# Selecting the routed rows of a sigmoid-attention and mixture-of-depths kernel: by ranks broadcast through DRAM and VectorE scans, in place of matmuls with a selection matrix

## Chip, cores and metric

One core of a Trainium2 chip runs the whole kernel in one launch. The metric is device time in microseconds, the median of several executions. Profiles come from one profiled execution each; its span is the time from the first to the last recorded event.

## What is computed

Attention with a sigmoid in place of the softmax, over 8 batches, 12 heads, 448 tokens and 64 values per head, all fp32. Its output, with the heads laid side by side (768 columns), is the input `x` of a mixture-of-depths block: in each batch the 128 tokens with the highest gate score go through a two-layer network, and the others pass unchanged.

```python
scores = scale * q @ k.T - log(S);  attn = 1 / (1 + exp(-scores));  x = attn @ v
gate = x @ w_gate                                    # per batch: 448 scores
top  = argpartition(-gate, capacity)[:capacity]      # capacity = 128
out  = x.copy()
out[top] = x[top] + sigmoid(gate[top])[:, None] * (relu(x[top] @ w1) @ w2)   # w1 768x1024, w2 1024x768
```

## The kernel before

**Attention.** The 96 heads are cut into 24 groups of four heads; group i belongs to batch i // 3. Two groups make a stage, so there are 12 stages (`s`), and a stage has seven units (`n` from 0 to 6). `turn` transposes raw q and k on VectorE (L184 to L191). `unit(s, n)` computes scores as 32-row by 64-column matmuls into PSUM (L209), and ScalarE evicts them through the sigmoid (L220) in two halves, four banks of PSUM being shared by successive units (`psc`). In a few early units the `o` banks are used instead. `values(s, n)` multiplies the attention weights of stage s by v (L250); its four parts run in the last unit of the stage and in units 0, 1 and 2 of the next one. After the fourth part, `take` transposes each pair of heads on VectorE into the row tile `x_b` (L265).

**The gate.** `gate_part` multiplies a group's rows by `w_gate` and sums (L272, L278). When a batch's three groups are done, `store` writes the row tile to a table `x_d` in DRAM with four transfers on the serial queue SP (L285), and `gate` builds a diagonal form of the scores (L294). `spread` turns that with one matmul by ones into a copy of all 448 scores on every partition (L304, L307) and also brings the scores into a per-token column (L309, L313). `rank` counts, for each token, the higher scores (L321) and the equal ones that stand earlier (L324). `place` adds the two counts (L330) and compares each rank with a row of 0 to 127, which gives a 0/1 matrix `sel` of tokens by slots (L333).

**Selection and routing.** `select` multiplies `sel` by columns that hold token number and score (L340, four matmuls with two result columns), into a spare corner of a score bank. `fetch` copies the token numbers out of PSUM (L345, L347), forms the gate's sigmoid on ScalarE (L349), and issues the gather of 128 rows from `x_d` on GpSimd's queue (L351). `turn_rows` transposes the gathered rows on TensorE (L361) and evicts them (L367). `ffn1` (L377, three pieces per batch, evicted with Relu at L379) and `ffn2` (L386, three pieces, each followed by L388 on VectorE) compute the network, and the result is scattered to the output by GpSimd (L392). `copy_out` copies the table `x_d` to the output on SP (L288).

**Order.** The order on every engine is the order of the program, written out by hand. `routed(b)` enters each batch's steps under a stage and unit in `late`, or in `beside`, which runs the selection inside a unit between its matmuls and its evictions. A batch's last group is computed in stage s - 1, and `spread` stands in unit 4 of stage s (unit 5 for batch 0), ranks in units 4 and 6, the selection in unit 1 or 0 of stage s + 1, and `turn_rows` in unit 3 of that stage. `gap(s, n)` runs the values, then from unit 3 on one waiting piece of `ffn1` or `ffn2` (`go`), and then what is due. After the 12 stages a tail without units finishes batches 6 and 7; `choose` selects there. Loads stand on SP in program order: v for the next stage at unit 0 and behind it up to five of 14 weight pieces at stages 1, 2 and 3 (`load_weights`), q and k at units 0 or 1 and 5. A load whose buffer is still read waits, and with it all that is behind it on SP.

Of the kernel before, what the change touches and what calls it, by code (L numbers as in the profile page):

```python
# [17 lines left out]
def kernel(  # L18
# [11 lines left out]
    nc = tc.nc  # L30
# [33 lines left out]
    head = ctx.enter_context(tc.tile_pool(name="head", bufs=2))  # L64
    dram = ctx.enter_context(tc.tile_pool(name="dram", bufs=2, space=bass.MemoryType.DRAM))
    attnp = ctx.enter_context(tc.tile_pool(name="attnp", bufs=1))
# [33 lines left out]
    def load_v(s):  # L100
# [15 lines left out]
        for n in range(4):  # L116
            nc.sync.dma_start(out=th[n * TT:(n + 1) * TT],
                              in_=blocks(4 * (n // 2), HK + n % 2, 4, 1))

    w1_sb = const.tile([P, KD, F], F32, name="w1_sb")  # L120
    w2_sb = const.tile([P, KF, D], F32, name="w2_sb")

    def load_weights(n0, n1):
        for n in range(max(n0, 0), min(n1, KD + KF)):
            if n < KD:
                nc.sync.dma_start(out=w1_sb[:, n], in_=moe_w1[n * P:(n + 1) * P, :])
            else:
                m = n - KD
                nc.sync.dma_start(out=w2_sb[:, m], in_=moe_w2[m * P:(m + 1) * P, :])
# [8 lines left out]
    earlier = const.tile([P, NC, S], mybir.dt.uint8, name="earlier")  # L138
    iota_r = const.tile([P, CAP], F32, name="iota_r")

    tok_gate = [const.tile([P, NC, 2], F32, name=f"tok_gate{n}") for n in range(2)]
    above = const.tile([P, NC], F32, name="above")
    level = const.tile([P, NC], F32, name="level")
    sel = const.tile([P, NC, CAP], F32, name="sel")

    def constants():
        nc.gpsimd.memset(ones, 1.0)
        make_identity(nc, iden)
        for a in range(4):
            p = slice(a * TT, (a + 1) * TT)  # L150
            nc.gpsimd.dma_start(
                out=wg_b[p],
                in_=bass.AP(tensor=moe_w_gate.tensor, offset=moe_w_gate.offset + a * TT,
                            ap=[[0, TT], [P, HP], [1, TT]]))
        nc.gpsimd.iota(iota_r, pattern=[[1, CAP]], base=0, channel_multiplier=0,
                       allow_small_or_imprecise_dtypes=True)
        for t in (above, level):
            nc.gpsimd.memset(t, 0.0)
        for t in tok_gate:
            nc.gpsimd.memset(t, 0.0)  # L160
            for a in range(4):
                nc.gpsimd.iota(t[a * TT:(a + 1) * TT, :, 0], pattern=[[4, NC]], base=a,
                               channel_multiplier=TB, allow_small_or_imprecise_dtypes=True)
        number = moe.tile([P, TB, TT], F32, name="rep")
        nc.gpsimd.iota(number, pattern=[[1, TB], [TB, TT]], base=0, channel_multiplier=0,
                       allow_small_or_imprecise_dtypes=True)
        for c in range(NC):
            nc.gpsimd.tensor_scalar(
                out=earlier[:, c, :], in0=number.rearrange("p r t -> p (r t)"),
                scalar1=tok_gate[0][:, c, 0:1], scalar2=None, op0=ALU.is_lt)  # L170

# [21 lines left out]
    def unit(s, n):  # L193
# [11 lines left out]
        for e in range(2):  # L205
            for y, (x, r) in enumerate(parts):
                for h in range(4):
# [5 lines left out]
                        start=(e == 0), stop=(e == 1))  # L213
        more = beside.pop((s, n), [])
        for fn, args in more:
            fn(*args, psc[0][:, 0, S:])
        for pr in range(2):
            a = attnp.tile([P, 2, S], F32, name=f"attn{pr}", bufs=NU + 3)
            attn[s, pr, n] = a
            nc.scalar.activation(a, psc[pr][:, :, :S], AF.Sigmoid, bias=bias_s, scale=QK_SCALE)  # L220
            if pr == 0:
                for fn, args in more:
                    fetch(*args, psc[0][:, 0, S:])

# [34 lines left out]
    def take(s, pr, x):  # L259

        b, g = divmod(2 * s + x, NG)
        if g == 0 and pr == 0:
            x_tiles[b] = rows_p.tile([P, TB, HP, TT], F32, name="x_b")
            gate_parts[b] = rows_p.tile([P, TB, NG], F32, name="gate_p")
        nc.vector.transpose(x_tiles[b][:, :, 2 * g + pr, :],  # L265
                            outs[s][x][:, pr, :S].rearrange("p (r t) -> p r t", t=TT))


    def gate_part(i):
# [8 lines left out]
        nc.vector.tensor_reduce(out=gate_parts[b][:, :, g], in_=tmp, axis=AX.X, op=ALU.add)  # L278

    def store(b):  # L280
        x_d = dram.tile([S, D], F32, name="x_d")
        st[b] = dict(x_d=x_d)
        view = x_d.rearrange("(t r) (h a d) -> a t r h d", r=TB, a=4, d=TT)
        for a in range(4):
            nc.sync.dma_start(out=view[a], in_=x_tiles[b][a * TT:(a + 1) * TT])  # L285

# [13 lines left out]
    def spread(b, where="o"):  # L300

        tg = tok_gate[b % 2]
        ps = banks(where)[:, 0, :S]
# [6 lines left out]
        for a in range(4):  # L310
            p = slice(a * TT, (a + 1) * TT)
            n = len(range(a, TB, 4))
            nc.vector.tensor_copy(tg[p, :n, 1], rep_t[p, a:TB:4, 0])  # L313
        st[b]["rep"] = rep

    def rank(b, c):
        tg, rep = tok_gate[b % 2], st[b]["rep"]
        n = P if c < NC - 1 else LAST
        own = tg[:n, c, 1:2]
        junk = moe.tile([P, S], F32, name="scr")  # L320
# [6 lines left out]

    def place(b):
        pl = moe.tile([P, NC], F32, name="place")
        nc.vector.tensor_add(pl, above, level)  # L330
        for c in range(NC):
            n = P if c < NC - 1 else LAST
            nc.vector.tensor_scalar(out=sel[:n, c], in0=iota_r[:n], scalar1=pl[:n, c:c + 1],  # L333
                                    scalar2=None, op0=ALU.is_equal)

    def select(b, s0, n, pk):

        tg = tok_gate[b % 2]
        for c in range(NC):
            nc.tensor.matmul(pk[:n, 0:2], sel[:, c, s0:s0 + n], tg[:, c, :],  # L340
                             start=(c == 0), stop=(c == NC - 1))

    def fetch(b, s0, n, pk):
        row = moe.tile([P, 1], I32, name="row", bufs=2)
        nc.vector.tensor_copy(row[:n], pk[:n, 0:1])  # L345
        idx = moe.tile([P, 1], I32, name="idx", bufs=2)
        nc.vector.tensor_scalar_add(idx[:n], pk[:n, 0:1], float(b * S))  # L347
        gt = moe.tile([P, 1], F32, name="gate", bufs=2)
        nc.scalar.activation(gt[:n], pk[:n, 1:2], AF.Sigmoid)  # L349
        xe = moe.tile([P, D], F32, name="xe", bufs=2)  # L350
        nc.gpsimd.indirect_dma_start(  # L351
            out=xe[:n], out_offset=None, in_=st[b]["x_d"][:, :],
            in_offset=bass.IndirectOffsetOnAxis(ap=row[:n, 0:1], axis=0))
        st[b].update(idx=idx, gate=gt, xe=xe)
# [56 lines left out]
    late = {}  # L411
    beside = {}

# [7 lines left out]
    def routed(b):  # L421

        s = (NG * b + NG - 1) // 2 + 1
        put(late, s, 5 if b == 0 else 4, spread, b)
        for c in range(NC - 1):
            put(late, s, 6 if b == 0 else 4, rank, b, c)
        put(late, s, 6, rank, b, NC - 1)
        put(late, s, 6, place, b)
        if s == NS:
            return  # L430
        put(late, *((s + 1, 1) if b == 0 else (s, 6)), copy_out, b)
        for s0, n in SLOTS:
            if s + 1 < NS:
                put(beside, s + 1, 1 if b == 0 else 0, select, b, s0, n)
            put(late, s + 1, 3, turn_rows, b, n)
            put(late, s + 1, 3, routed_groups, b, n)

    def gates(i):
        gate_part(i)
        b, g = divmod(i, NG)  # L440
        if g == NG - 1:
            store(b)
            gate(b)

    def gap(s, n):
# [13 lines left out]
        due(late, s, n)  # L459
        if n == 3 and s > 0:  # L460
            gates(2 * s - 1)

    def stream():
# [3 lines left out]
        load(1)  # L467
        nc.vector.memset(sel, 0.0)
        nc.vector.memset(bias_s, NEG_LOG_S)
# [4 lines left out]
        for _ in range(3):  # L474
            nc.tensor.matmul(warm[:, 0], sel[:, 0, :], sel.rearrange("p c n -> p (c n)"),  # L475
                             start=True, stop=True)
        constants()
        for s in range(NS):
            for n in range(NU):
# [4 lines left out]
                if n == 0:  # L484
                    load_v(s + 1)
                    load_weights(5 * s - 5, 5 * s)
                if s == 0 and n == 1:
# [3 lines left out]
                gap(s, n)  # L491
                if n == NU - 2:
                    turn(2 * s + 2)
                    load(2 * s + 4)

        def choose(b):
            for s0, n in SLOTS:
                pk = banks("psc")[:, 0]
                select(b, s0, n, pk)
                fetch(b, s0, n, pk)  # L500

        choose(B - 2)
        for n in range(5):
            gap(NS, n)
        for n in range(3):
            go("any")
        due(late, NS, NU - 1)
        choose(B - 1)
        copy_out(B - 1)
        while len(ready) > 1:  # L510
            go("any")
# [3 lines left out]
        while ready:  # L515
            go("any")
        assert not late and not beside

# [31 lines left out]
```

## Time and profile before

| | |
|---|---|
| Median of 3 runs | 490.42 us (489.97 to 491.16) |
| Profiled execution | 489.37 us |
| Its span | 487.6 us |
| TensorE matmuls busy | 470.9 us (97%) |
| VectorE, ScalarE, GpSimd busy | 211.7, 189.4, 28.0 us |
| DMA | 68.67 MB, mean 141 GB/s |
| Scores L209 in `psc` / values L250 with raw_v | 150.3 / 134.7 us |
| `ffn1` L377 / `ffn2` L386 in the `o` banks | 81.7 / 73.4 us |
| Selection L340 | 64 records, 8.3 us |
| `sel` L333 on VectorE | 32 instructions, 7.6 us |
| Gather L351, issue to landing | median 4.5 us |
| Table L285, issue to landing | median 6.7 us, 32 issues |

Shares are of the span. fp32 matmuls appear as two records each. "PEld" is the loading of weights into TensorE, which overlaps its matmuls. The chain of work that ended last goes back from the last instruction to what released each step; it says where a saved microsecond would shorten the execution. The row of granted clock shows in tenths of full speed what the clock gate let TensorE have. A DMA's time to landing counts from its issue to the completion that others wait for.

### The profile page before, as it was taken

To read this page: it belongs to the slowest core of one execution; us is meant where nothing else is said; L and a number is where in the kernel's file an instruction comes from. 1 tells how busy PE (TensorE), PEld (TensorE's weight loads), DVE (VectorE), ACT (ScalarE), POOL (GpSimd) and SP (SyncE) were. 2 spreads that over 40 slices of the span, in tenths; PEclk is the share of its full clock that TensorE was granted. 3 is DMA by queue.
4 is the path that set the end of the run, shared out by engine and by line. 5 is a ranking of instruction groups with operands and counts; after the bars stand their busy time and mean duration, and the time that the engine had idled before them with its cause. 6 is when DMAs were issued, how large, how long until landed. Compare 5 with 4: busy or idle time off the path is not lost.

```text
span 487.6 us, 14593 instructions
## 1 busy us (share of the span) xinstructions
PE 470.9 (97%) x6662; PEld 309.5 (63%) x6662; DVE 211.7 (43%) x461; ACT 189.4 (39%) x253; POOL 28.0 (6%) x45
## 2 busy tenths in 40 slices
PE   8998999499999999999999999999999999999995
PEld 3554646386568465577567476568576667489994
DVE  4315296508252168268152156456433355184101
ACT  4746464223442453544352552543343445011010
POOL 8000000000000000010000000010000000001000
PEclk9999999789999999999999999999999999999999
DMA  8929298985463078498262075658632036165000
GB/s 264 198 83 336 107 311 137 304 249 104 176 152 109 3 166 155 169 221 202 99 153 99 13 173 95 223 131 167 214 82 82 35 59 172 34 97 182 14 34 32
DMA packets 117277, 68.67 MB, mean 141 GB/s; under 512 B 95648, under 2 KB 108000, under 8 KB 116960
## 3 DMA queue, kind: packets, MB, share of 16 engines
q1 hardware_dynamic: 115808, 61.35, 49.0%
q0 software_dynamic: 1408, 6.39, 4.3%
q8 instruction: 52, 0.85, 0.7%
q14 instruction: 9, 0.07, 0.0%
HBM read 53.58 MB, written 25.17 MB: 161 GB/s over the span
## 4 chain that ended last, share of the span: by engine, by line
PE 85%; issue 4%; DMA 3%; DVE 3%; SPq 2%; ACT 1%; POOLq 0%; DVEq 0%; ACTq 0%
PE o L250 24%; PE psc L209 24%; PE o L377 16%; PE o L386 13%; SPq L285 2%; PE o L209 2%; DMA x_d<-x_b 1%; PE psc L386 1%; DMA xe<-x_d,row 1%; PE psc L340 1%; PE o L304 1%; PE o L361 1%; PE o L475 1%; DVE x_b L265 1%; PE psc L377 1%
## 5 line engine op out<-in xcount | busy, mean ns | idle before, releaser
L220 ACT ACTIVATE attn<-psc,bias_s 128x896 f32<-128x896 f32 x158 | 151.1, 1003 | 130.6 <-PE psc L209 117.3
L209 PE MATMUL psc<-qT,kT 32*64 32x448 f32 x2528 | 150.3, 540 | 1.9 <-ACT attn L220 1.9
L250 PE MATMUL o<-attn,raw_v 32*64 32x448 f32 x2304 | 134.7, 536 | 0.7 <-ACT o L253 0.7
L209 PEld LDWEIGHTS psc<-qT,kT 32*64 32x64 f32 x2528 | 61.5, 131 | 61.1 <-issue 37.4
L250 PEld LDWEIGHTS o<-attn,raw_v 32*64 32x64 f32 x2304 | 60.3, 132 | 48.6 <-issue 38.8
L377 PEld LDWEIGHTS o<-xeT,w_sb 128*128 128x128 f32 x672 | 78.9, 197 | 10.7 <-issue 7.9
L377 PE MATMUL o<-xeT,w_sb 128*128 128x128 f32 x672 | 81.7, 282 | 0.9 <-ACT xeT L367 0.9
L386 PE MATMUL o<-w_sb,hT 128*128 128x256 f32 x320 | 73.4, 383 | 0.0
L265 DVE STREAM_TRANSPOSE x_b<-o 128x448 f32<-128x448 f32 x48 | 26.9, 618 | 106.9 <-PE o L250 83.7
L386 PEld LDWEIGHTS o<-w_sb,hT 128*128 128x128 f32 x320 | 59.4, 190 | 16.8 <-issue 5.8
L184 DVE STREAM_TRANSPOSE kT<-raw_k 128x384 f32<-128x384 f32 x48 | 24.7, 554 | 30.2 <-DMA raw_k<-in_k_dram 15.0
L388 DVE SCALAR_TENSOR_TENSOR xe<-o,gate,xe 128x256 f32<-128x256 f32 x20 | 9.7, 483 | 51.5 <-PE o L386 51.5
L379 ACT ACTIVATE hT<-o 128x384 f32<-128x384 f32 (+1 forms) x21 | 9.5, 454 | 56.9 <-PE o L377 56.9
L278 DVE TENSOR_REDUCE gate_p<-scr 128x14 f32<-128x896 f32 x24 | 26.1, 1087 | 0.8
L250 PE MATMUL o<-attn,raw_h 32*64 32x448 f32 x384 | 26.4, 534 | 0.0
L272 DVE TENSOR_TENSOR scr<-x_b,wg_b 128x896 f32<-128x896 f32 x24 | 25.6, 1067 | 0.1
L191 DVE STREAM_TRANSPOSE qT<-raw_q 128x896 f32<-128x896 f32 x23 | 24.7, 1074 | 1.9 <-DMA raw_q<-in_q_dram 1.9
L351 POOL DMA_INDIRECT xe<-x_d,row x8 | 7.9, 987 | 297.0 <-DVE idx L347 222.8
L324 DVE SCALAR_TENSOR_TENSOR scr<-rep,tok_gate,earlier 128x448 f32<-128x448 f32 (+1 forms) x32 | 21.8, 683 | 1.1
L321 DVE TENSOR_SCALAR_CACHE_REDUCE scr<-rep,tok_gate 128x448 f32<-128x448 f32 (+1 forms) x32 | 21.4, 669 | 0.9
L309 DVE STREAM_TRANSPOSE scr<-o 128x448 f32<-128x448 f32 x8 | 5.2, 650 | 37.6 <-ACT rep L307 37.6
L253 ACT ACTIVATE o<-bias_s 1x1 f32<-1x1 f32 x36 | 5.9, 165 | 36.8 <-PE o L250 24.9
(56 smaller groups left out, 204.7 us busy)
## 6 DMA issues: line engine op xcount, KB each, us to landing
raw_k<-in_k_dram SPq DMA_DIRECT2D x24, 448.0 KB, 4.6
raw_q<-in_q_dram SPq DMA_DIRECT2D x24, 448.0 KB, 4.5
x_d<-x_b SPq DMA_DIRECT2D x32, 336.0 KB, 6.7
out_dram<-x_d SPq DMA_DIRECT2D x8, 1344.0 KB, 9.0
raw_v<-in_v_dram SPq DMA_DIRECT2D x48, 192.0 KB, 3.9
w_sb<-in_moe_w_dram SPq DMA_DIRECT2D x6, 512.0 KB, 6.1
w_sb<-in_moe_w_dram SPq DMA_DIRECT2D x8, 384.0 KB, 5.2
raw_h<-in_v_dram SPq DMA_DIRECT2D x48, 32.0 KB, 5.5
```

Of the source, the lines that this page charges most:

```text
L184: nc.vector.transpose(kT[i][:, e, :HK], sk[:, e, :HK].rearrange("p (m c) d -> p c m d", c=NF))
L191: nc.vector.transpose(qT[i], sq)
L209: nc.tensor.matmul(psc[h // 2][y * Dh:(y + 1) * Dh, h % 2, :S], kT[2 * s + x][d, e, r:r + 2, :].rearrange("d r t -> d (r t)"), qT[2 * s + ...
L220: nc.scalar.activation(a, psc[pr][:, :, :S], AF.Sigmoid, bias=bias_s, scale=QK_SCALE)
L250: nc.tensor.matmul(o[x][j * Dh:(j + 1) * Dh, pr, :S], w, a[rows, j, :], start=(n == 0 and c == 0), stop=(n == 3 and c == NF - 1))
L265: nc.vector.transpose(x_tiles[b][:, :, 2 * g + pr, :], outs[s][x][:, pr, :S].rearrange("p (r t) -> p r t", t=TT))
L272: nc.vector.tensor_tensor(out=tmp, in0=x_tiles[b][:, :, 2 * g:2 * g + 2, :].rearrange("p r h d -> p r (h d)"), in1=wg_b[:, 2 * g:2 * g + 2 ...
L278: nc.vector.tensor_reduce(out=gate_parts[b][:, :, g], in_=tmp, axis=AX.X, op=ALU.add)
L321: nc.vector.tensor_scalar(out=junk[:n], in0=rep[:n], scalar1=own, scalar2=0.0, op0=ALU.is_gt, op1=ALU.add, accum_out=above[:n, c:c + 1])
L324: nc.vector.scalar_tensor_tensor(out=junk[:n], in0=rep[:n], scalar=own, in1=earlier[:n, c, :], op0=ALU.is_equal, op1=ALU.mult, accum_out=l ...
L377: nc.tensor.matmul(ps[:, f - f0, :n], w1_sb[:, t, f * P:(f + 1) * P], xeT[:, t, :n], start=(t == 0), stop=(t == KD - 1))
L386: nc.tensor.matmul(ps[:n, :ND], st[b]["hT"][:, t, :n], w2_sb[:, t, cols], start=(t == 0), stop=(t == KF - 1))
```

## The change

- `place` keeps only the add. It stores the 448 ranks to a small DRAM tile with GpSimd's queue (128 partitions of four single values) and reads them back from there, the same row to all 128 partitions, into `spot`.
- `select` is no matmul any more. VectorE compares `spot` with the slot number of each partition and sums token numbers (from `number`, int16) and scores (from `rep`) in two scans with an accumulator; then come the copies, the gate and the gather as before, now from SBUF.
- `beside` and `choose` are gone. Ranking and placing stand together in unit 4 (unit 5 for batch 0), the selection in unit 1 of the next stage. Batch 0's `turn_rows` and network begin in unit 4 and not 3.
- `store` is gone: `take` stores each pair of heads as soon as it is transposed, 4 transfers of 448 pieces of 128 B, 16 per stage; `x_d` has three buffers.
- In stage 2, the `turn` for the next stage moves from unit 5 to unit 3, and a `gate_part` from unit 3 to unit 6.
- Weights are loaded 3, 6, 2 and 3 pieces at a time, behind units (1, 0), (1, 5), (2, 0) and (3, 1), and not 5, 5 and 4 at unit 0 of stages 1 to 3.
- Constants on GpSimd change accordingly, and the first matmuls use a zeroed scratch tile of the same width as `sel`.

On TensorE the order of what stays differs only around batches 0 to 4, where pieces of the network fall one unit later or earlier; on GpSimd's queue each batch's two rank transfers stand ahead of its gather, and in the tail ahead of the scatter of batch 5.

```diff
+    WEIGHTS = {(1, 0): (0, 3), (1, NU - 2): (3, 9), (2, 0): (9, 11), (3, 1): (11, KD + KF)}
...
-        more = beside.pop((s, n), [])
-        for fn, args in more:
-            fn(*args, psc[0][:, 0, S:])
...
-            if pr == 0:
-                for fn, args in more:
-                    fetch(*args, psc[0][:, 0, S:])
...
+        rows = st[b]["x_d"].rearrange("(t r) c -> t r c", r=TB)
+        for a in range(4):
+            c = hp * P + a * TT
+            nc.sync.dma_start(out=rows[:, :, c:c + TT],
+                              in_=x_tiles[b][a * TT:(a + 1) * TT, :, hp, :])
...
-    def store(b):
-        view = x_d.rearrange("(t r) (h a d) -> a t r h d", r=TB, a=4, d=TT)
-        for a in range(4):
-            nc.sync.dma_start(out=view[a], in_=x_tiles[b][a * TT:(a + 1) * TT])
...
         nc.vector.tensor_add(pl, above, level)
-        for c in range(NC):
-            n = P if c < NC - 1 else LAST
-            nc.vector.tensor_scalar(out=sel[:n, c], in0=iota_r[:n], scalar1=pl[:n, c:c + 1],
-                                    scalar2=None, op0=ALU.is_equal)
-    def select(b, s0, n, pk):
-        for c in range(NC):
-            nc.tensor.matmul(pk[:n, 0:2], sel[:, c, s0:s0 + n], tg[:, c, :],
-                             start=(c == 0), stop=(c == NC - 1))
+        ranks = dram.tile([NC, P], F32, name="ranks")
+        nc.gpsimd.dma_start(out=ranks.rearrange("c p -> p c"), in_=pl)
+        spot = moe.tile([P, S], F32, name="spot")
+        nc.gpsimd.dma_start(out=spot, in_=bass.AP(tensor=ranks.tensor, offset=ranks.offset,
+                                                  ap=[[0, P], [1, S]]))
+        st[b]["spot"] = spot
+    def select(b, s0, n):
+        picked = []
+        for what in (number.rearrange("p r t -> p (r t)"), st[b]["rep"]):
+            got = moe.tile([P, 1], F32, name="got", bufs=4)
+            junk = moe.tile([P, S], F32, name="scr")
+            nc.vector.scalar_tensor_tensor(
+                out=junk[:n], in0=st[b]["spot"][:n], scalar=slots[s0][:n], in1=what[:n],
+                op0=ALU.is_equal, op1=ALU.mult, accum_out=got[:n, 0:1])
+            picked.append(got)
...
-        for c in range(NC - 1):
-            put(late, s, 6 if b == 0 else 4, rank, b, c)
-        put(late, s, 6, rank, b, NC - 1)
-        put(late, s, 6, place, b)
+        for c in range(NC):
+            put(late, s, 5 if b == 0 else 4, rank, b, c)
+        put(late, s, 5 if b == 0 else 4, place, b)
...
-                put(beside, s + 1, 1 if b == 0 else 0, select, b, s0, n)
-            put(late, s + 1, 3, turn_rows, b, n)
-            put(late, s + 1, 3, routed_groups, b, n)
+            put(late, s + 1, 1, select, b, s0, n)
+            put(late, s + 1, 4 if b == 0 else 3, turn_rows, b, n)
+            put(late, s + 1, 4 if b == 0 else 3, routed_groups, b, n)
...
-        if n == 3 and s > 0:
+        if n == (NU - 1 if s == 2 else 3) and s > 0:
             gates(2 * s - 1)
...
-                if n == NU - 2:
+                if n == (NF if s == 2 else NU - 2):
                     turn(2 * s + 2)
                     load(2 * s + 4)
+                load_weights(*WEIGHTS.get((s, n), (0, 0)))
```

## The prediction

> **What bounds the kernel now.** I read the busy shares first, then the row of granted clock, then TensorE's waits, and last the chain of work that ended last, in order of time.
>
> ```profile
> PE 470.9 (97%) x6662; PEld 309.5 (63%) x6662; DVE 211.7 (43%) x461; ACT 189.4 (39%) x253; POOL 28.0 (6%) x45
> PEclk9999999789999999999999999999999999999999
> ```
>
> TensorE is busy almost all the time at full clock, but for one dip in slices 8 and 9 (85 to 110 us). So only two things count: matmuls that are removed, and stretches in which TensorE waits or runs slowly. Its waits name the dip (columns: us in total, times, longest):
>
> ```profile
> PE o L361 <- DMA xe<-x_d,row: 5.9, 1, 5.9
> ```
>
> TensorE sat idle once, before the first batch's row transposes (L361), for the gathered rows. The chain shows what lay before and after (start us, us, what):
>
> ```profile
> 78.53 7.14 DMA x_d<-x_b
> 85.73 0.81 issue
> 86.54 6.74 DMA xe<-x_d,row
> 93.42 1.53 PE o L361 x6
> 94.97 0.82 ACT xeT L367
> 95.83 6.62 PE o L377 x36
> 102.46 1.69 PE psc L209 x32
> 104.14 4.21 PE o L377 x36
> 108.36 0.75 PE o L304 x2
> ...
> 121.83 1.50 PE psc L209 x31
> 123.33 0.98 PE psc L340 x8
> 124.32 3.19 PE o L250 x64
> ...
> 157.88 3.01 PE o L250 x63
> ```
>
> The table x_d landed at 85.7, the gather at 93.3. The first 36 matmuls after the wait took 6.62 us, the same 36 later 4.21. The clock in steps (stretch, length, busy PE, PEld, DVE, ACT, POOL, granted clock, DMA share, GB/s):
>
> ```profile
> 87.50:90.50 3.00, 0.01 (x2) 0.00 (x0) 2.93 (x5) 1.90 (x2) 0.15 (x1) 1.00 1.09 235
> 90.50:93.40 2.90, 0.00 (x0) 0.01 (x1) 2.80 (x4) 0.00 (x0) 0.00 (x0) 0.51 1.16 222
> 93.40:100.80 7.40, 6.48 (x29) 6.10 (x30) 0.20 (x1) 0.81 (x1) 0.00 (x0) 0.50 1.09 416
> ```
>
> After 3.0 us without matmuls the clock was halved, and stayed so for 10.3 us. The slow part cost (6.62 - 4.21) + (1.53 - 0.66, the transposes in other stages) = 3.3 us on top of the wait. The Trainium skill, "TensorE: Matmul & The Clock Gate", Part 1, lets a halved clock recover after about 3.4 us of busy matmuls; this row shows 7.4 us, and the row is used. By the page the slow part would cost an estimated 1.7 us and the gain below would be 1.6 us smaller.
>
> **Matmuls removed.** Each select (L340, 8 records) takes 0.98 us of the chain, and the value matmuls behind it take 3.19 instead of 3.01 us: 1.16 us per batch for batches 1 to 6. Batch 7's at 446.43 takes 0.79. All lie on the chain, so for batches 1 to 5 nothing can take their place unless the rows come late. They don't: there ranks are placed in unit 4 of one stage and used in unit 1 of the next, over 15 us of units later, and the gather has from unit 1 to unit 3 (9 us by the chain: 1.50 + 2.25 + 1.55 + 2.25 + 1.53) where its landing took 3.9 to 5.4 us. Sum for 1 to 5: **-5.8 us**.
>
> **The new chain: ranks to selection.** In place of the matmuls stands: ranks stored by GpSimd (512 elements of 4 B), read back to 128 partitions (128 rows of 1,792 B), two VectorE scans, a gather. No row of before shows either transfer. Call L the time from the end of the add at L330 to the landed broadcast. Nearest rows (last column: us from issue to landing):
>
> ```profile
> xe<-x_d,row POOLq DMA_INDIRECT x8, 4.5
> out_dram<-xe,idx POOLq DMA_INDIRECT x8, 3.3
> wg_b<-in_moe_w_gate_dram POOLq DMA_DIRECT2D x4, 24.0 KB, 6.2
> ```
>
> Quiet, one transfer of this queue lands in 3.0 us (the scatters after 425 us); under heavy load it took 7.2 (the longest of xe). So L lies between 2 x 3.0 + 0.2 = 6.2 and 2 x 7.2 + 0.2 = 14.6. I take 4.2 for the ranks (3.3, and 0.9 more on GpSimd: 192 pieces of wg_b took it 0.65 us, so 512 may take 1.7) and 3.3 for the broadcast, with 0.3 for semaphores: **L = 7.8**, near the lower end because the serial queue (SP) is stuck then, see below. The skill speaks against such a store: "DMA: Bandwidth & Descriptors", Rules for kernel authors, says a non-contiguous last dimension becomes one descriptor per element. The same page (Anatomy of one DMA) gives some 2.0 us fixed plus bytes, which would make L an estimated 4.5 and the total that of the first rival; no row here has 4-byte pieces.
>
> The scans cost 2 x (0.685 + 0.083, the L324 row with its accumulator read) = 1.5 us, the two small copies and semaphores 0.6: the gather is issued 2.1 us after the broadcast. On VectorE the four L333 instructions (0.87 us) go, so its load hardly moves. Behind the scans, VectorE holds the x_b transposes, and ScalarE, which waits for the gate's scan, holds the next sigmoid evictions: that is the added wait.
>
> **Batch 0.** Ranking moves from stage 2, unit 6 to unit 5, and the transposes before it (turn, 2.4 us) to unit 3, where they take the slot of a gate_part (2.2 us) that goes behind. Ranks began at 71.75 behind turn; now they begin when the copies of spread end (69.6), take 5.7 and the add ends at 75.5. Broadcast at 83.3, gather issued at 85.4. The table is no longer late: pairs are stored as they come, 16 issues per stage. An issue of a small transfer took SP 0.47 us (raw_h, 4 in 1.87), so 7.5 us from 65; batch 0's eight come first and land near 74, ten us before they are needed. Behind them SP waits at the v load for stage 4, whose buffer is freed only at about 85 (it was issued at 86.12 before), so nothing loads the engines between 75 and 85; the copy to the output and the last weights are still behind it. Then the gather meets those loads: 6 us (4.5 to 6.7), landing at 91.4.
>
> TensorE would reach unit 3 at 84.5 (85.6 less the select). ScalarE's evictions resume at 85.1, so unit 3 starts at 86.1, unit 4 at 89.0 (an eviction between two units without filler) and ends at 90.9; transposes from 91.4 to 92.1. Now spread stands ahead of the first ffn1: its diagonal is ready 7.5 us after the x_b transposes begin (86.12 to 93.6 before; now 85.2 to 92.7). Spread to 93.4, ffn1 to 97.65, the second ffn1 4.2 more: 101.85, with the same work done as at 109.11 before: **-7.3 us**. The idle pieces (1.6, 0.9, 0.5, 0.6 us) are each below the 3.0 us after which the clock fell.
>
> **Batches 6 and 7.** No units cover these. Batch 6: the add ends 8.7 us after its spread starts (405.96 to 414.68), the gather lands 8.7 + 7.8 + 2.1 + 3.9 = 22.5 after it, and TensorE comes to L361 at 23.4 - 1.16 = 22.25: -1.16 + 0.25 = **-0.9**. Batch 7: the add ends at 443.2, the broadcast lands at 451.0, gate at 452.7. ScalarE's Relu for the third ffn1 group of batch 6 stands behind that gate, so hT comes at 453.2, while ffn2 needs it at 451.8 (449.2 plus six eighths of 3.46): a stall of 1.4. Then 0.9 + 3.46 us of ffn2 to 457.55; the gather lands at 453.1 + 3.9 = 457.0, in time. L361 began at 456.75: **+0.8**. GpSimd's scatter of batch 5 now waits behind the broadcast; batch 7's gather reuses its buffer, and it lands near 452, before the gather is issued.
>
> **Weights and the rest: 0.** Three pieces instead of five at stage 1 and six in its unit 5 lie where DMA was 56% busy (30 to 60 us); first use of w1 is at 93. The last three, behind the copy to the output, land near 103 and are used by ffn2 after 120. If they were late, ffn2 of batch 0 waits. Startup changes (a smaller memset target, iotas) lie beside the loads. Cost between -0.5 and +1.
>
> **Sum.** -5.8 - 7.3 - 0.9 + 0.8 = -13.2. The profiled execution took 489.37 us (span 487.6 and 1.8 around it): 476.2. The median of the runs shown is 1.05 higher, 490.42, which gives 477.2; I forecast **477**.
>
> **Rivals.**
> 1. The round trip is short (L about 6.2). Then batch 0 still waits for its diagonal (92.1): -7.9; batches 6 and 7 lose no time: -1.16 and -0.8. Sum -15.7, **474.7**. For it: 3.0 us rows in a quiet queue. Against: 512 pieces of 4 B.
> 2. L about 10. Batch 0 -5.1, batch 6 +1.3, batch 7 +2.8: -6.8, **483.6**, and up to 489 if the waits of 3.6 to 3.8 us halve the clock (3.3 us each).
> 3. Slower: the round trip takes the place of the stall, at the same spot and twice in the tail. With L = 12, ScalarE's gate holds unit 3 until 90.3 (5.8 us idle, clock halved): -1.9; batch 6 waits 4.4 and batch 7 5.6 us, each with 3.3 of slow clock: +6.6 and +8. With -5.8: +7, **497**. It decides from L about 10.3. For it: 7.2 us for a loaded gather. Against: SP is stuck in that stretch, and DMA is quiet at 443 to 452, since the copy to the output starts as soon as the pairs have landed (near 435, not 445).
> 4. The finer stores choke SP: 192 issues at the x_d row's median of 2.7 us would be 518 us. Against: that time is back-pressure of 336 KB each (4 in 8.8 us at about 150 GB/s), the shortest took 0.56. At 0.56 a stage of 35 us has 9 us of stores. If each took 1.5, loads would come late and the time would be near **495**.
>
> **How the numbers follow.** Forecast (L 7 to 9) 0.55, rival 1 0.17, rival 2 0.14, rival 3 0.09, rival 4 0.05. The range goes from a little below rival 1 to the upper end of rival 2 without the clock, widened for dips: 472 to 487. A measurement here can tell about 0.3% (1.5 us) from no change: faster 0.84, same 0.03, slower 0.13.
>
> **What will show it.** Right: no L340 on the chain; POOL's gather of batch 0 ended by VectorE, not by x_d; no half clock at 85 to 110; two new POOL issues that land in about 4.2 and 3.3 us; a wait of ScalarE for VectorE at the gate near 83 and 451. Wrong: landings of 5 us or more, TensorE idle over 3 us at batch 0, 6 or 7, or a new dip in PEclk.

## The result and the profile after

The changed kernel took 542.48 us (median of 4 runs, 540.46 to 544.77) against 490.20 for the kernel before: ratio 1.107 (95% interval 1.102 to 1.112). It is slower by 52 us; the forecast was 477, faster, with a range up to 487. The profiled execution took 543.21 us, its span 541.3. Times below are medians of all runs of a kernel, and its profile is of one of them; the four runs of `e11_hybrid` alone fell into two groups, 477.1 and 477.8 us against 484.6 and 484.7 us at a lower mean granted clock, and its profile is of the first group.

The page after, busy shares and granted clock (to be laid beside the two rows that open the prediction):

```profile
PE 487.3 (90%) x6598; PEld 317.1 (59%) x6598; DVE 216.1 (40%) x461; ACT 189.1 (35%) x253; POOL 38.9 (7%) x57
PEclk9999998699999998999799997999699999899798
```

There are 64 matmul records (8.3 us) fewer, as the change says, and yet TensorE is busy 16.4 us longer, while the clock row now has dips along the whole span and not one. Of the 53.7 us that the span grew, 16.4 are busy time of TensorE (what is left runs some 24.7 us slower) and 37.3 are idle time of it.

Who waits for what in the changed kernel (us in total, times, longest):

```profile
DVE scr L343 <- DMA spot<-ranks: 102.6, 8, 16.7
POOL spot L333 <- DMA ranks<-place: 71.0, 7, 11.7
ACT gate L352 <- DVE scr L343: 39.0, 5, 11.7
PE psc L214 <- ACT attn L222: 12.1, 5, 9.0
```

This is the new path read from its source on: GpSimd waits for the stored ranks before it can read them back (L333), VectorE waits for the broadcast in front of its scans (L343), ScalarE waits for the scans with the gate's sigmoid (L352), and TensorE waits for the evictions behind that gate. The chain that ended last shows the same at batch 2, where the prediction had seen no danger (start, us, what):

```profile
194.82 0.17 DVE place L329
...
195.28 10.37 DMA ranks<-place
...
206.20 9.81 DMA spot<-ranks
...
216.03 0.70 DVE scr L343 x2
...
217.49 0.20 ACT gate L352
...
218.64 2.65 PE psc L214 x32
```

From the end of the add to the landed broadcast lie 21.0 us here (194.99 to 216.0), where the prediction had L = 7.8. At batch 0 it was 16.6 (the add ended at 75.4, where 75.5 was forecast; the scans began at 91.95), in the quiet tail 14.6 and 14.3 (450.6 to 465.2, and 487.1 to 501.4). The unit behind it took 2.65 us, not 1.5 to 1.7, at a granted clock of 1.00: its second half waited for ScalarE's second eviction. Just before, from 213.4 to 216.9 us, the clock had been halved again, after TensorE had been idle from 211.4 us on. The transfers themselves (from the same kernel's list of issues; last column us from issue to landing, the median of those whose landing the trace shows):

```profile
spot<-ranks POOLq DMA_DIRECT2D x8, 224.0 KB, 7.2
ranks<-place POOLq DMA_DIRECT2D x8, 2.0 KB, 8.8
```

2 KB take longer than 224. The 8.8 is the landing of the last of the eight stores, the only one shown; in all eight, GpSimd issues the read-back 9.3 to 12.6 us after the store. The broadcast took 3.6 us at batch 0 and 4.7 in the tail, near the forecast of 3.3, and up to 9.7 in the stages. At least in the tail it is not traffic that makes the store wait. The stretch from the issue of the ranks to the issue of the read-back in batch 7 (length, then busy time of PE, PEld, DVE, ACT, POOL, granted clock, DMA share, GB/s):

```profile
487.40:496.70 9.30, 8.51 (x66) 7.85 (x64) 0.12 (x1) 0.49 (x1) 0.79 (x1) 1.00 0.02 0
```

The DMA engines are 2% busy, almost nothing else moves, and the store still takes 9 us (in batch 6 it was 4%, and as long).

### The profile page after: what moved, and what is told of

Read it like the earlier page. It is cut to its first block, busy times and chain, and to the rows that moved or that the text cites. A ratio compares the mean times of both kernels' runs of the same rounds, so it can differ in the third digit from the quotient of the medians.

```text
span 541.3 us, 14701 instructions
## 1 busy us (share of the span) xinstructions
PE 487.3 (90%) x6598; PEld 317.1 (59%) x6598; DVE 216.1 (40%) x461; ACT 189.1 (35%) x253; POOL 38.9 (7%) x57
## 4 chain that ended last, share of the span: by engine, by line
PE 68%; DMA 14%; issue 8%; DVE 6%; ACT 3%; POOLq 0%; DVEq 0%
PE psc L214 22%; PE o L249 19%; PE o L380 12%; PE o L389 11%; DMA ranks<-place 7%; DMA spot<-ranks 4%; ACT attn L222 2%; DVE scr L319 2%; PE o L214 2%; DVE scr L322 2%; PE o L364 1%; PE o L302 1%; DMA xe<-x_d,row 1%; DVE scr L343 1%; DMA raw_k<-in_k_dram 1%
## 5 line engine op out<-in xcount | busy, mean ns | idle before, releaser
L214 PE MATMUL psc<-qT,kT 32*64 32x448 f32 x2528 | 169.2, 564 | 17.7 <-ACT attn L222 12.1
L249 PE MATMUL o<-attn,raw_v 32*64 32x448 f32 x2304 | 152.0, 559 | 12.8 <-issue 11.7
L214 PEld LDWEIGHTS psc<-qT,kT 32*64 32x64 f32 x2528 | 67.9, 136 | 84.0 <-issue 46.0
L249 PEld LDWEIGHTS o<-attn,raw_v 32*64 32x64 f32 x2304 | 69.9, 137 | 64.1 <-issue 50.9
L380 PE MATMUL o<-xeT,w_sb 128*128 128x128 f32 x672 | 79.2, 277 | 1.1 <-ACT xeT L370 1.0
L343 DVE SCALAR_TENSOR_TENSOR scr<-spot,slot,number 128x448 f32<-128x448 f32 x8 | 5.5, 685 | 102.6 <-DMA spot<-ranks 102.6
L189 DVE STREAM_TRANSPOSE kT<-raw_k 128x384 f32<-128x384 f32 x48 | 24.7, 552 | 29.0 <-PE psc L214 15.4
L249 PE MATMUL o<-attn,raw_h 32*64 32x448 f32 x384 | 31.2, 550 | 0.2 <-issue 0.2
L196 DVE STREAM_TRANSPOSE qT<-raw_q 128x896 f32<-128x896 f32 x23 | 24.7, 1075 | 8.6 <-DMA raw_q<-in_q_dram 8.6
L331 POOL DMA_DIRECT2D ranks<-place x8 | 6.5, 817 | 241.5 <-DVE place L329 241.5
L389 PE MATMUL psc<-w_sb,hT 128*128 128x256 f32 x64 | 15.8, 399 | 7.5 <-ACT hT L382 7.5
L322 DVE SCALAR_TENSOR_TENSOR scr<-rep,score,earlier 128x448 f32<-128x448 f32 (+1 forms) x32 | 21.9, 683 | 1.1
```

The source lines that it names most:

```text
L189: nc.vector.transpose(kT[i][:, e, :HK], sk[:, e, :HK].rearrange("p (m c) d -> p c m d", c=NF))
L196: nc.vector.transpose(qT[i], sq)
L214: nc.tensor.matmul(psc[h // 2][y * Dh:(y + 1) * Dh, h % 2, :S], kT[2 * s + x][d, e, r:r + 2, :].rearrange("d r t -> d (r t)"), qT[2 * s + ...
L249: nc.tensor.matmul(o[x][j * Dh:(j + 1) * Dh, pr, :S], w, a[rows, j, :], start=(n == 0 and c == 0), stop=(n == 3 and c == NF - 1))
L322: nc.vector.scalar_tensor_tensor(out=junk[:n], in0=rep[:n], scalar=own, in1=earlier[:n, c, :], op0=ALU.is_equal, op1=ALU.mult, accum_out=l ...
L343: nc.vector.scalar_tensor_tensor(out=junk[:n], in0=st[b]["spot"][:n], scalar=slots[s0][:n], in1=what[:n], op0=ALU.is_equal, op1=ALU.mult, ...
```

## Experiments

The first theory was A: the store of 512 four-byte ranks takes some 9 us and holds the transfer engines, while the rest of the change is good. Rivals were B, the 16 small stores per stage or the spread weights choke SP, and C, any round trip through DRAM by GpSimd's queue costs some 14 us, whatever its pieces.

**Selection by matmuls again, all else as changed** (`e1_matsel`): `select`, `fetch` and `sel` are as in the kernel before; ranks still in unit 4 or 5, pairs stored as they come, weights spread.

> The changed kernel with the selection by matmuls put back; stores by pairs, spread weights, earlier ranking and batch 0's later start stay. Theory A (the store of 512 four-byte ranks takes about 9 us and holds the transfer engines; the rest of the change is good): batch 0 no longer waits for its table, 480 to 485 us. Theory B (the finer stores and the weights' order choke SP and the loads): 515 us or more. Theory C (any round trip through DRAM by GpSimd's queue takes some 14 us, whatever its pieces): as A, 480 to 485.

Measured 485.52 us, ratio to before 0.991 (0.988 to 0.995), half a microsecond above the range of A and C. B falls: pair stores, earlier ranking and weights together are no harm, they bring 4 to 5 us, and the whole loss sits in the new selection.

**Ranks in rows of 16 B** (`e2_rows16`):

```
-  ranks = dram.tile([NC, P]);  dma_start(out=ranks.rearrange("c p -> p c"), in_=pl)
+  ranks = dram.tile([P, NC]);  dma_start(out=ranks, in_=pl)        # 128 pieces of 16 B
   spot  = the row of 512 ranks to every partition
   scans read spot, number and rep as (c, p) views of 512 columns
```

> The changed kernel with the ranks stored as 128 pieces of 16 B, one per partition, and read back in that order (the scans walk the broadcast row with a stride, over 512 columns in place of 448). Theory A: the store lands in 3.5 to 5 us, the broadcast in 4 to 5, no stall of several us is left: 476 to 484 us. Theory B: 515 us or more. Theory C: the store still lands in 8 to 9 us and the time stays above 520.

Measured 486.63 us, ratio 0.991 (0.988 to 0.994). The layout of a 2 KB transfer is worth 56 us, although the broadcast and the scans are longer here: C falls, and A holds but for 2.6 us over its range. The list of issues of this kernel:

```profile
spot<-ranks POOLq DMA_DIRECT2D x8, 256.0 KB, 4.8
ranks<-place POOLq DMA_DIRECT2D x8, 2.0 KB, 1.7
```

The store lands in 1.7 instead of 8.8 us (6.5 and 3.1 for batches 0 and 1, under load), and the broadcast, though it is now 256 KB, in 4.8 instead of 7.2. But 477 is not reached either; that is taken up below.

**A dense store that nobody reads, in the kernel before** (`e3_store`): one store in `place`, `ranks.rearrange("c p -> p c")` stored from `pl`, no reader.

> The kernel before plus one store of the 512 ranks per batch that nobody reads or waits for (extra work). If such a store holds the engines for other transfers (part of theory A), the table of batch 0 and the gathers of batches 0, 6 and 7 come up to 9 us later: 494 to 510 us. If it is slow only for itself (theory C): 489 to 492.

Measured 511.76 us, ratio 1.045 (1.041 to 1.049), 1.8 us over the top of what A gave. So the store costs time without anybody waiting for it. The gather in this kernel's list of issues:

```profile
xe<-x_d,row POOLq DMA_INDIRECT x8, 7.4
```

The gather, behind a store that lands in 9.4 us, takes 7.4 where it took 4.5, and TensorE waits 10.1 us for it at batch 0, where it waited 5.9.

**Transfers alone** (`probe`, then `e7_probe`).

> Transfers alone, with nothing else in flight; attention and routing are left out, and the output is a copy of q. Time from issue to landing on GpSimd's queue, three times each. Theory A: 512 pieces of 4 B to DRAM about 9 us, 128 pieces of 16 B 2.5 to 4, 128 of 4 B in one 512 B row 3 to 5; beside the 512 pieces, three loads of 448 KB on SP land some 6 to 9 us later than alone, beside the 16 B pieces at most 1 us later. Theory C: 7 to 9 us for every shape, and the loads land as when alone. If the pieces' number decides and not their neighbourhood, 512 pieces set 512 B apart take as long as dense ones; if neighbours in a line wait for each other, 2.5 to 4 us.

In the first of the two, the copy from q to the output ran beside the first half, so only the rest of it can be read: 9.4 us for the dense store and 4.0 for rows of 16 B, both beside loads, and 3.5 for 512 pieces of 4 B written into SBUF and not into DRAM. The second did one transfer at a time.

> Transfers alone, one after the other, each waiting for the last; attention, routing and FFN are left out (the output is a copy of q). From issue to landing: a store of 512 pieces of 4 B to DRAM 8 to 10 us by GpSimd's queue and by SP's (if it is the form and not the queue), of 1,024 pieces 16 to 19, of 128 pieces of 4 B 3 to 4, if each piece costs some 17 ns; 128 pieces of 16, 64 and 256 B 2 to 3 us each, if it is the number of pieces under some size and not the bytes. If 4 B is slow only where neighbours in DRAM share a line, 512 pieces that lie 512 B apart take under 5 us. Three loads of 448 KB take 10 to 14 us alone, as long beside the store of 128 x 16 B, and at least 5 us longer beside the store of 512 x 4 B if that store holds the engines.

Its list of issues, with the size telling which is which (2.0 KB dense is 512 pieces, 0.5 KB is 128, 4.0 KB is 1,024; `apart` is 512 pieces of 4 B at a distance of 512 B):

```profile
dense<-vals POOLq DMA_DIRECT2D x2, 2.0 KB, 9.1
rows<-vals POOLq DMA_DIRECT2D x2, 2.0 KB, 1.7
dense<-vals POOLq DMA_DIRECT2D x2, 0.5 KB, 8.2
dense<-vals POOLq DMA_DIRECT2D x2, 4.0 KB, 9.2
apart<-vals POOLq DMA_DIRECT2D x2, 2.0 KB, 2.2
```

The estimate of 17 ns per piece (9 us over 512) falls: 128 dense pieces cost 8.2 us and 1,024 cost 9.2, so the number hardly counts. The same 512 pieces cost 2.2 us when they lie apart. The queue is not it either, since the same store from SP took 11.1 us. What costs is that neighbouring words of 4 B in DRAM are written by different pieces. By the trace's records of single transfers, three loads of 448 KB moved in 4.6 us alone (less than expected), in 4.8 beside the store in rows, and in 7.8 to 8.3 beside the dense one: 3.2 to 3.7 us longer, where at least 5 was expected.

The same records show where the time lies. For the 512 dense pieces issued at 1.34 us they run from 3.1 to 3.5 us, and the landing was seen at about 10.4; so no engine is recorded as busy for 9 us, and most of the time passes behind the last record. Beside the dense store, 7 to 10 of the 384 pieces of the loads took 1.5 to 4.2 us each, where none took over 1.1 alone, and the others (median 0.14) moved as before. So "holds the transfer engines" in theory A is too wide: a few pieces are held, and a load lands only with its last piece.

**The same, in the kernel** (`e13_apart`): the kernel before with an unread store of 512 pieces per batch, 512 B apart.

> The kernel before with an unread store of the 512 ranks per batch, each 4 B piece 512 B from the next in DRAM, where dense pieces had cost 21.3 us. If the cost is that neighbours of 4 B in DRAM are written by several engines at once (alone, 512 pieces apart landed in 2.2 us, dense in 9.1, and 128 dense ones in 8.2): 488 to 493 us. If it is the number of pieces: 505 to 515 us.

Measured 491.87 us, ratio 1.003 (1.001 to 1.005), where the dense pieces had given 1.045. The distance alone takes away some 19 of 21 us.

**Which engine hands the wait on?** (`e8_gate_late`, `e5_dense_late`.) Theory G: ScalarE, which stands at the gate with all evictions behind it. Rival V: VectorE, which stands at the scans with the x_b transposes behind it.

```
 in select:     -  gt = sigmoid(picked[1])
 in turn_rows:  +  gt = sigmoid(got)        # after the eviction into xeT
```

> The changed kernel with its dense store; only ScalarE's sigmoid of the gate stands after the eviction of the row transposes instead of in the selection. Theory G: ScalarE, held 39 us at the gate with the sigmoid evictions behind it, is what hands the late broadcast on to TensorE; without it 505 to 525 us (not under the 511 less 6 of the kernel before with the dense store added, since the store still slows other transfers). Rival V: VectorE waits 103 us for the broadcast with the x_b transposes behind it, which free the banks that the next values need, so TensorE stands as long: 535 to 543 us.

Measured 539.87 us, ratio 1.100 (1.092 to 1.108): 2.6 us less than the change by the medians, with intervals that overlap, and inside V's range. G falls. ScalarE's wait at the gate is gone from the profile, VectorE's is the same, and TensorE now waits for the gather (and 10.0 us more once, in another bank). So the wait is handed on, but the path that V named, the banks that the x_b transposes free, is not among the waits that the profile names for TensorE:

```profile
DVE scr L343 <- DMA spot<-ranks: 100.4, 8, 16.2
PE o L362 <- DMA xe<-x_d,row: 12.6, 2, 7.2
```

The other test gave the selection more room, by a unit (batches 0 to 5: unit 2 and 4 in place of 1 and 3 or 4).

> The changed kernel with its 512-piece store of the ranks, selections of batches 0 to 5 one unit later (unit 2 instead of 1) and their row transposes in unit 4. Theory latency: the 56 us that the dense store costs are mostly VectorE and ScalarE held by the late broadcast; one unit more (about 4.5 us) for six batches takes 4 to 5 us off each wait and several half-clock stretches with it: 505 to 520 us. Rival contention: the store slows all other transfers (the kernel before lost 21.3 us to it with nobody waiting for the ranks), so moving the selection changes little: 530 to 545 us.

Measured 554.94 us, ratio 1.133 (1.125 to 1.141), worse than either theory had it. One unit later, the scans stand on VectorE behind the last values' transposes and a `gate_part`, so the broadcast is there in time, but ScalarE, which comes to the gate early, waits longer (39.0 us in 5 times before the edit):

```profile
ACT gate L352 <- DVE scr L343: 63.9, 8, 11.9
```

More room for a transfer is no gain if the step that uses it moves behind other work of an in-order engine while its own follower stays in front of work on the next.

**How much is the wait, how much the hold?** (`e12_rows_spare`: rows of 16 B for the round trip, and an unread dense store behind it.)

> Ranks stored in 128 pieces of 16 B and read back so, as in the run that took 486.6 us, and behind the broadcast's issue a second, unread store of the same ranks in 512 pieces of 4 B. It splits the 56 us that the dense store cost: what this kernel loses is the hold on other transfers, the rest is VectorE and TensorE waiting for late ranks. By the kernel before with an unread dense store (+21.3 us) 504 to 512 us; if the waits are nearly all of it, 489 to 495; if the hold on transfers is nearly all, 530 to 543.

Measured 531.47 us, ratio 1.080 (1.075 to 1.086). That is 45 of the 56 us, at the lower edge of the range given for the hold on transfers being nearly all of it. It does not split them cleanly, because the dense store is issued just behind the broadcast and holds it too: in the profiled execution (534.57 us) the broadcast took 9.0 us instead of 4.8 and VectorE waited 48.6 us for it, against 32.7 with the short store alone. What it shows is that most of the loss comes even when nobody waits for the dense store itself; how much of it goes through the late broadcast and how much through other transfers is not shown.

**Batch 0 with a short store** (`e4_rows16_late0`, `e9_rows16_gate`, `e10_rows16_gate_w`). With 486.6 us, the short store gained 4 us instead of 13. Its chain pointed at batch 0, where TensorE waited 5.8 us in one piece for evictions behind the gate (8.8 for evictions in the whole kernel) and then ran 10.2 us at half clock. Three edits tried to mend it: selection of batch 0 two units later; the late gate of above; and with it the weights as before.

> The kernel with ranks stored in 128 pieces of 16 B, and batch 0 alone selected in unit 3 and turned in unit 5 of its stage, instead of 1 and 4. Theory P: what was missing of the forecast there was cover at batch 0 (TensorE waited 5.8 us in one piece for evictions behind the gate, then ran 10.2 us at half clock, which costs some 3 to 5). With two units more (over 8 us) before the selection the wait and the dip at 92 to 102 us go, values(3,0) comes 7 to 10 us earlier than in that kernel, less what the four pieces cost that now find no slot in that stage (0 to 3): 478 to 482 us. Rival Q: the pair stores or the scans over 512 strided columns cost the time, wherever the selection stands: 484 to 488 us.

> Ranks stored in 128 pieces of 16 B, selection where the change has it, and the gate's sigmoid after the eviction of the row transposes. Theory G: the 5.8 us that TensorE waited at batch 0 for evictions behind the gate go, with the half clock of 10 us after them (3 to 5), and 1 to 4 us in the tail: 477 to 481 us, near the blind forecast. Rival V: VectorE still waits for the broadcast in front of the x_b transposes, so the stall is only renamed: 484 to 487 us.

> As the run with 16 B pieces and the late gate, with the weights loaded five pieces a stage as before. With matmul selection this gave 484.0 after 485.5 us with the spread loads, in another call. If the spread puts loads beside batch 0's round trip and gather, 1 to 2 us less than that run; if it is even, the same within 1 us; if the spread helps, 1 to 3 us more.

Measured 485.73 (ratio 0.993, 0.990 to 0.996), 484.26 (0.991, 0.988 to 0.994) and 485.27 (0.991, 0.988 to 0.995): the first two miss the theory that a single stall had to go and lie in the ranges of their rivals, and the third shows no effect of the weights that is clear of the spread. The chain of the second shows why (the end of the add for batch 0 is at 75.90):

```profile
76.18 5.36 DMA ranks<-place
...
81.84 3.81 DMA spot<-ranks
...
85.74 1.17 DVE scr L349 x2
...
88.21 2.15 DVE x_b L268 x4
...
95.65 1.86 PE o L305 x2
97.51 5.79 PE o L388 x36
```

Even the short store takes 5.4 us here, under load, and the round trip 9.8 us. VectorE reaches the x_b transposes at 88.2 and has 7.4 us of work from there to the end of the next batch's diagonal, which the prediction knew; `spread` stands ahead of `ffn1`, so TensorE waits for VectorE, the clock halves, and 36 matmuls take 5.79 us. Moving one wait brings up the next.

**Weights as before, selection by matmuls** (`e6_matsel_weights`).

> Selection by matmuls as before, pair stores as in the change, but the weights loaded five pieces a stage as before. With the spread loads it took 485.5 us. Theory pair stores: the gain of 5 us over the kernel before is that the row table is no longer late at batch 0; the time stays at 484 to 487.5 us. Theory weights: the gain is the spread of the weights' loads; the time goes back to 488.5 to 491 us.

Measured 484.00 us, ratio 0.990 (0.983 to 0.996), so the 4 to 5 us belong to the pair stores and the earlier ranking, which no run separates, and not to the weights. Its row of granted clock is nines from end to end.

**Each batch by what covers it** (`e11_hybrid`, `e14_hybrid0`). `BY_MATMUL` batches use `sel` and `select` of the kernel before, the others the scans with rows of 16 B and the late gate.

```
+  BY_MATMUL = (0, 6, 7)          # e14: (0,)
   place:  if b not in BY_MATMUL: store ranks in rows of 16 B, read back;  else: build sel
   routed: if b not in BY_MATMUL: put(late, s + 1, 1, scan, b, ...);       else: put(beside, ..., select, ...)
```

> Batches 0, 6 and 7, which have few or no units to cover a round trip, are selected by matmuls as before; batches 1 to 5 by VectorE from ranks stored in 16 B pieces, with the late gate; weights as before, pair stores. If the gains of the steps add up, it is 484.0 us (all by matmuls, weights as before) less 5 x 1.16: 477 to 480 us. If the selects that go from batches 1 to 5 are only replaced by another wait, 482 to 485 us.

> Only batch 0 is selected by matmuls; batches 1 to 7 by VectorE from ranks in 16 B pieces, with the late gate. The kernel with batches 0, 6 and 7 by matmuls took 481.2 us. The blind steps gave -0.9 for batch 6 and +0.8 for batch 7, together 0: 480 to 482.5 us. If the last round trips, with no units beside them, stall the tail by a few us: 483.5 to 487 us.

Measured 481.18 us, ratio 0.984 (0.976 to 0.992), and 481.60 us, ratio 0.984 (0.980 to 0.987). The first median is 1.2 us above its first theory's range and below its rival's; the second is in the range of its first theory. The profiled execution of the first took 477.12. Its page:

```profile
PE 462.4 (97%) x6622; PEld 299.0 (63%) x6622; DVE 221.0 (46%) x472; ACT 188.9 (40%) x253; POOL 34.7 (7%) x58
PEclk9999999999999999999999999999999999999999
```

No dip is left in this execution, and both versions are faster than the kernel before and the changed one: the longest run of either took 484.8 us, the shortest of the kernel before beside them 487.3.

## Why the prediction was wrong

The starts of the first value matmul of a stage (us, from one profiled execution each) carry most of the points. "Matmuls" is `e6_matsel_weights`, "rows" is `e2_rows16`, "hybrid" is `e11_hybrid`. The execution of "rows" is the longest of its six (488.75 us) and holds a stretch of half clock at 44 us, described at the end, that cost it some 1.5 us:

| stage | before | changed | matmuls | rows | hybrid |
|---|---|---|---|---|---|
| 3 | 118.62 | 121.11 | 108.88 | 118.81 | 108.86 |
| 5 | 190.28 | 197.29 | 184.55 | 192.77 | 182.74 |
| 11 | 412.76 | 448.65 | 405.95 | 410.50 | 400.11 |
| span | 487.6 | 541.3 | 480.8 | 486.9 | 475.3 |

- **The step that failed is the size of L.** The prediction put the ranks' store at 4.2 us and the broadcast at 3.3. They took 8.8 and 7.2; L was 14 us with next to nothing else moving and 17 to 21 in the stages. The larger part of the miss is the store: with the DMA quiet, the broadcast took 4.7. The issue of the store took GpSimd 0.8 us (0.6 for rows), so the 0.9 that was added there for the number of pieces was not where the time went. The store's bounds came from the gather, the scatter and `wg_b`, whose pieces are wide; the one thing that was new, words of 4 B side by side in DRAM, stood in no row, and the value was chosen near the lower end because traffic would be low. In the quiet tail traffic was not the cause. The stated upper bound of 14.6 was also too low for every batch in the stages.
- **The rule of the Trainium skill that was weighed there** ("DMA: Bandwidth & Descriptors", Rules for kernel authors: a last dimension that is not contiguous becomes one descriptor per element) pointed at the right line, and its advice held. The number of pieces was not the price, though: 128 dense pieces cost 8.2 us, 1,024 cost 9.2 and 512 apart 2.2. The page's Specifications table says that below 512 B the engine reads, modifies and writes. That would fit pieces that share a block of DRAM and wait for one another; against it as a full account, rows of 16 B share such blocks too and landed in 1.7 us. No run here shows which it is.
- **A cost that no step had: the store holds other transfers.** Unread, it cost the kernel before 21 us; behind a short round trip it cost 45. The prediction priced the store only for who waits for it.
- **"Batches 1 to 5: the rows don't come late"** failed with L. At batch 2, VectorE had nothing else to do from 200.6 us on and waited until 216.0. With the short store the step holds: from stage 3 to stage 11 the hybrid needs 291.25 us and the matmul version 297.07, 5.82 less, where the prediction said 5.8 (5 selects of 1.16); both profiles are at full clock there.
- **Batch 0, -7.3.** 1.2 of that was the select. Keeping the matmuls, the earlier ranking and the pair stores brought 5.7 us by stage 5 (184.55 against 190.28), where 6.1 was forecast: this part of the working was good in that execution. In the profile of `e1_matsel`, the same with the weights spread, only 0.9 us are gained there (189.39): TensorE waits 2.7 us for VectorE from 131.4 us on and then runs 3.4 us at half clock, which the other does not. With the round trip there, it was eaten up even with the short store (+2.5 in rows, some 1.5 of it from the stretch at 44 us; 2.5 gained with the late gate), since L is 10 to 11 there and not 7.8.
- **Batches 6 and 7, together -0.1.** 481.60 against 481.18 us with and without the scans there: no difference that these runs can tell, and no test of the -0.1 either.
- **Weights, 0.** Right as far as the times tell, in both pairs of kernels (medians 1.5 and 1.0 us apart). **SP is not choked** (against rival 4): right as well.
- **The clock.** The prediction took idle pieces below 3.0 us as harmless. In the changed kernel the clock fell at 213.4 us, 2.0 us after TensorE's last matmul, and in `e1_matsel` 2.8 us after it, so 3.0 us was the length of one gap and no bound.
- **Rival 3** named the right way (the round trip in place of the stall, a gate that holds evictions, half clock after idling) and had 0.09 of the chances. It gave 497 for L = 12 at batch 0 and the tail alone; VectorE waited for the broadcast in batches 1 to 5 too (8.3 us at batch 1, 15.1 to 16.7 at the others), and the hold on the other transfers came on top. The gate was only the last link: without it the time fell by 2.6 us.

What stays open is how the 56 us divide between held transfers and late ranks. By the kernel before with an unread store it would be 21 and 35, by the changed order with one 45 and 11; the orders differ, and in the second the broadcast was among what was held. Why dense words in DRAM take 8 to 9 us was not settled either: the runs show the condition, and that most of the time lies behind the engines' records, but not the mechanism.

## What to carry to other kernels

Before a small intermediate goes through DRAM, look at how wide its contiguous pieces are there, and price the transfer also for what it does to all others in flight: here 2 KB in another layout were worth 56 us. Where a trace has no row like the new transfer, the nearest row is no bound; give the unknown a wide range and measure that one transfer first. A step that waits on a round trip belongs only where units cover it, and is better chosen batch by batch than for all of them.

## What the runs showed of the hardware

- 128, 512 and 1,024 dense pieces of 4 B to DRAM landed in 8.2, 9.1 and 9.2 us, 512 of them 512 B apart in 2.2, 128 of 16 B (and of 64 and 256 B) in 1.7. In SBUF, 512 pieces of 4 B landed in 3.5, in the first probe. The engines' records of the dense stores end within some 2.5 us of the issue; the rest of the 8 to 9 us passes before the landing is seen.
- The halved clock came in stretches of 3.4, 6.8, 10.2 or 13.7 us, seven of them in the changed kernel before its last instructions.
- In five of the profiled executions, of different kernels, the clock was halved for 3.4 us from 43 to 44 us on, and not in the others, although all have the same wait of TensorE before it (1.4 us, up to about 42). The stretch from 44.0 to 47.5 us of `e2_rows16` (columns as above):

```profile
44.00:47.50 3.50, 3.50 (x48) 1.77 (x41) 0.06 (x1) 1.85 (x2) 0.00 (x0) 0.52 1.01 362
```

In `e9_rows16_gate`, with the same program there, the same stretch has a granted clock of 1.00 and 82 matmul records, not 48: some 1.5 us of difference between two profiles that no edit explains. Why the clock fell there in some executions only is not known.
